# The order of an attention and two-MoE kernel's middle part, planned anew with other costs for issues, transfers and small matmuls

## The chip, the cores and the metric

The kernel runs on one core of a Trainium2 chip. The metric is the device time of one execution in microseconds (us). TensorE (PE in the profile) does the matmuls, VectorE (DVE) and ScalarE (ACT) the elementwise work, GpSimd (POOL) and SyncE (SP) issue the transfers (DMAs).

## The reference

Three stages follow each other: a retention recurrence over 4 x 8 heads of 768 steps, a feed-forward layer with `h * sigmoid(1.702 h)` between two products, and a second one with a rational function between them.

```python
for t in range(S):
    state = gamma[None, :, None, None] * state + np.einsum('bhd,bhe->bhde', k[:, :, t], v[:, :, t])
    y[:, :, t] = scale * np.einsum('bhd,bhde->bhe', q[:, :, t], state)
...
h = x @ w_in
g = h * (1.0 / (1.0 + np.exp(-1.702 * h)))
return (g @ w_out).astype(np.float32)
...
h = x @ w_in
h2 = h * h
h3 = h2 * h
P = a[0] + a[1] * h + a[2] * h2 + a[3] * h3
Q = 1.0 + np.abs(b[0]) * np.abs(h) + np.abs(b[1]) * h2
g = P / (Q + 1e-06)
return (g @ w_out).astype(np.float32)
```

x is 3072 x 512, `w_in` 512 x 2048 and `w_out` 2048 x 512, float32 throughout.

## The kernel before

**Stages.** The recurrence is computed in 24 chunks of 128 steps of the flattened sequences. For a chunk c the queries and keys are loaded with 16 strided DMAs each (the queries on SP, the keys on POOL, from `in_q` and `in_k`) into buffers of the tags `turnq`, `turnk`, `rawk` and `rawv`, scaled and transposed on VectorE into `qT` and `kT`. TensorE makes the scores (`scores`), VectorE masks them (`masks`, tile `sm`), TensorE adds the products with the values and with the running state (`st`), and the sums go on as inputs of the first layer. The buffers of a tag are reused: a tile takes the one whose last use lies longest back, so that a buffer that held chunk c's keys takes another chunk's queries or keys, and the later load waits for the earlier tile's last reader. A trace shows a buffer under the name of its first tile with `_slot` behind it: `rawk_slot` may hold queries.

Both layers split float32 into a rounded high part and a low rest (`gh` and `gl`, `xh` and `xl`), so that three products of 128 x 128 by 128 x 512 stand for one. In the first layer a step j makes `hp` (four inputs' products), ScalarE the activation `z`, ScalarE and VectorE its parts `gh{j}` and `gl{j}`, and TensorE the output products `o`. The outputs are copied out of PSUM into `os` or `sumb` by ScalarE and VectorE and stored to `x2`, to be read again by the second layer. In the same time the second layer's weights are brought in and split: a weight half `s2_n` (n from 0 to 31) is loaded on SP from `moe2_w_in` or `moe2_w_out` into a buffer of `os`, `sumb` or `a`, ScalarE and VectorE make `u{n}` and sums of them, and the results are stored to DRAM on POOL (`wc0_...`, `wo...`). The second half of the planned part combines blocks of inputs and weights (`xs`, `x0`, `split` from a `ring` of loaded weights) for the last part.

**What sets the order.** Each engine and each DMA queue works through its instructions in the order in which the program gives them. The order of the first steps (the string `ORDER`, with `FIRST_STEPS = 14`) is written out by hand. From step 14 on the program doesn't issue: a class `Deck` records every operation with its reads and writes, and `flush` issues all of them in the order that `plan` gives (all of these instructions carry line 375 in the profile, and in the changed kernel 378). This part runs from about 126 to 606 us of the span. The last part, `layer2`, again has an order of its own in the source (line 390).

`plan` is a list scheduler. Each engine has a time from which it is free (`free`, at the start 0 for all five). Of an engine's operations whose inputs are ready, the one recorded first is taken; of the engines, the one that can start first. An operation takes what `cost` says: a matmul of 512 columns 0.2267 us, a smaller one 0.0178 us per 64 columns, a DMA's issue 0.4 us on SP and 0.7 us on POOL, VectorE's and ScalarE's operations a constant and a part by their size. `nc.group(0.25)` makes one operation of several matmuls and adds 0.25 us. A DMA moves behind those before it (`moving`), and its data count as landed 1.6 us later:

```python
            if op.run is not None:
                size, run = op.run
                ns = next((y for x, y in self.RUNS if x >= run), 0.176)
                moving = max(moving, t + 1.0) + size / run * ns / 16
                op.end = moving + 1.6
```

`size` is the DMA's bytes and `run` its contiguous bytes, 128 for the strided loads. These costs decide the order and nothing else: no engine waits for a planned time, but for what its instruction reads and writes. The functions `att_S`, `y_unit` and `z_unit` are the three places where groups are made: scores of the first planned chunk, the first and the second half of a chunk with the next chunk's scores.

Of the kernel before, what the change touches and what calls it, by code (L numbers as in the profile page):

```python
# [233 lines left out]
class Deck:  # L234
# [46 lines left out]
    def cost(self, engine, method, out, views):  # L281
        if method == "dma_start":
            size = 1
            for v in views[:1]:
                size = v.at.size * (P // ROWS if v.home.space != "dram" else 1)
            return (0.4 if engine == "sync" else 0.7), size * 4
        n = int(np.prod(out.shape[1:])) if isinstance(out, View) else 64
        if engine == "tensor":
            return (0.2267 if n >= 512 else 0.0178 * n / 64), None
        if engine == "scalar":  # L290
            return 0.19 + n * 0.00083, None
        if method == "tensor_scalar":
            return 0.155 + n * 0.00052, None
        return 0.155 + n * 0.00104, None
# [19 lines left out]
    def plan(self):  # L314
        ops = self.ops
        left = []
        for line in self.lines.values():
            line.place(ops)
        for op in ops:
            for x in op.need:  # L320
                ops[x].wake.append(op.n)
            left.append(len(op.need))
        free = dict.fromkeys(("tensor", "vector", "scalar", "gpsimd", "sync"), 0.0)
        wait = {e: [] for e in free}
        ready = {e: [] for e in free}
        moving = 0.0
# [5 lines left out]
        while done < len(ops):  # L332
            best = None
            for e in free:
                if ready[e]:
                    t = free[e]
                elif wait[e]:
                    t = max(free[e], wait[e][0][0])
                else:
                    continue  # L340
                if best is None or t < best[0]:
                    best = (t, e)
            t, e = best
            while wait[e] and wait[e][0][0] <= t + 0.02:
                heapq.heappush(ready[e], heapq.heappop(wait[e])[1])
            op = ops[heapq.heappop(ready[e])]
            op.start = t
            free[e] = t + op.dur
            if op.run is not None:
                size, run = op.run  # L350
                ns = next((y for x, y in self.RUNS if x >= run), 0.176)
                moving = max(moving, t + 1.0) + size / run * ns / 16
                op.end = moving + 1.6
            else:
                op.end = t + op.dur
            order.append(op)
            done += 1
            for x in op.wake:
                left[x] -= 1
                if not left[x]:  # L360
                    o = ops[x]
                    r = 0.0
                    for y in o.need:
                        p = ops[y]
                        gap = 0.05 if p.run is not None else 0.0 if p.engine == o.engine else 0.35 if p.engine == "tensor" else 0.2
                        r = max(r, p.end + gap)
                    heapq.heappush(wait[o.engine], (max(r, t), x))
# [442 lines left out]
def tile_kernel(ctx: ExitStack, tc: tile.TileContext, q, k, v, w1i, w1o, w2i, w2o, pa, pb, cst, out):  # L810
# [480 lines left out]

    def att_S(c, tg, alt=None, sums=True):
        pss = [ps(tg[n], f"pS{n}_{c}").rearrange("a x t -> a (x t)") for n in range(2)]
        with nc.group(0.25):
            scores(c, pss, 0, 0)
        if sums:
            state_sums(c, pss, {(x, n) for x in range(2) for n in range(2)})
# [233 lines left out]
        return [t[:, 0], t[:, 1]], None, 0  # L1531

    def y_unit(c):
        with nc.group(0.25):
            att_Y0(c, ("a", "a"), *out_home(c), True, PIECES)
        PIECES[c][0]()
        states_of(c, PY[c])
# [6 lines left out]
    def z_unit(c):  # L1544
        py = PY.pop(c)
        _, second, outs, lows = PIECES.pop(c)
        with nc.group(0.25):
            second()
            if c + 1 < NT // P:
                scores(c + 1, py, 4 * D, 1)  # L1550
# [566 lines left out]
```

## Time and profile before

| | us |
|---|---|
| median of 3 runs | 1106.44 |
| lowest and highest | 1106.31, 1108.31 |
| the profiled execution | 1104.64 |
| its span, first to last instruction | 1102.8 |
| TensorE busy | 1087.5 (99%) |
| VectorE busy | 872.2 (79%) |
| ScalarE busy | 698.5 (63%) |
| GpSimd busy | 208.0 (19%) |
| DMA, mean rate | 181 GB/s |

All durations and places below are of the profiled execution, with times from the start of its span; the time outside the span is 1104.64 − 1102.8 = 1.8 us. Busy is the share of the span in which an engine had an instruction running; a row of a timeline gives start, length, engine, source line, operation, output and inputs and, in brackets, how long the engine had stood idle before it and what released it.

### The profile page before, as it was taken

How to read it: one execution, taken by the hardware profiler on the slowest of the kernel's cores; microseconds unless marked ns; L12 is line 12 of the kernel's file. 1: busy time of each engine (PE TensorE's matmuls, PEld its weight loads, DVE VectorE, ACT ScalarE, POOL GpSimd, SP SyncE). 2: the span in 40 equal slices, each digit the busy share in tenths (PEclk: the TensorE clock that was granted, in tenths of full speed). 3: DMA queues.
4: the chain of work that ended last, by engine and by line, in shares of the span. 5: the costliest groups of instructions: out<-in, count | busy, mean ns of one | idle time of the engine just before them, and what ended most of it. 6: DMA issues, size and time to landing. Idle time of an engine off the chain costs nothing.

```text
span 1102.8 us, 19408 instructions
## 1 busy us (share of the span) xinstructions
PE 1087.5 (99%) x7169; PEld 883.0 (80%) x7169; DVE 872.2 (79%) x1262; ACT 698.5 (63%) x1105; POOL 208.0 (19%) x368
## 2 busy tenths in 40 slices
PE   8999999999999999999999999999999999999998
PEld 6678878888877778888888888888888888888886
DVE  6898556356745679789995799998988897899895
ACT  5898422233323346667763788787787886787882
POOL 0003346545675601133102000000000000000000
PEclk9999999999999999999999999999999999999999
DMA  9964336546776775798878775832454913454011
GB/s 229 318 174 131 77 113 165 141 103 153 194 195 158 219 233 200 236 364 311 290 254 329 267 247 202 315 153 86 126 153 130 333 51 96 124 162 117 19 39 39
DMA packets 192703, 199.76 MB, mean 181 GB/s; under 512 B 108512, under 2 KB 140768, under 8 KB 192608
## 3 DMA queue, kind: packets, MB, share of 16 engines
q1 hardware_dynamic: 172960, 154.45, 46.7%
q0 software_dynamic: 19648, 44.06, 11.5%
q8 instruction: 57, 0.93, 0.4%
q14 instruction: 38, 0.31, 0.1%
HBM read 139.73 MB, written 58.72 MB: 180 GB/s over the span
## 4 chain that ended last, share of the span: by engine, by line
PE 78%; POOL 5%; DMA 5%; SPq 5%; issue 3%; DVE 1%; ACT 1%; DVEq 0%; POOLq 0%; ACTq 0%
PE o L390 26%; PE o_slot L375 14%; PE hp_slot L375 13%; PE a L390 12%; PE c L390 6%; SPq L390 3%; PE b L390 3%; PE hp L390 3%; POOL turnk_slot L375 2%; SPq L375 2%; POOL rawk_slot L375 2%; POOL rawv_slot L375 2%; PE pS_slot L375 1%; DMA os_slot<-in_moe_w_in_dram 1%; DMA s<-in_moe_w_out_dram 1%
## 5 line engine op out<-in xcount | busy, mean ns | idle before, releaser
L375 PE MATMUL o_slot<-gh_slot,wo 128*128 128x512 f32 x480 | 161.7, 393 | 0.0
L375 PEld LDWEIGHTS o_slot<-gh_slot,wo 128*128 128x128 f32 x480 | 90.1, 188 | 19.3
L375 ACT ACTIVATE z_slot<-hp_slot 128x512 f32<-128x512 f32 x56 | 33.4, 596 | 107.8 <-PE hp_slot L375 107.8
L390 PE MATMUL a<-x,wi 128*128 128x512 f32 x384 | 97.5, 389 | 0.0
L375 PE MATMUL o_slot<-gl_slot,wo 128*128 128x512 f32 x240 | 93.5, 390 | 0.0
L375 POOL DMA_DIRECT2D turnk_slot<-in_k_dram x144 | 80.3, 559 | 60.7 <-DVE kT_slot L375 38.7
L375 PE MATMUL hp_slot<-xh_slot,wi 128*128 128x512 f32 x256 | 85.3, 394 | 0.0
L375 PE MATMUL hp_slot<-xl_slot,split_slot 128*128 128x512 f32 x336 | 84.7, 389 | 0.0
L390 PEld LDWEIGHTS a<-x,wi 128*128 128x128 f32 x384 | 72.1, 188 | 15.0
L390 DVE SCALAR_TENSOR_TENSOR z<-z,ab,w 128x1024 f32<-128x1024 f32 x48 | 61.5, 1280 | 28.4 <-ACT w L390 28.4
L375 PEld LDWEIGHTS hp_slot<-xl_slot,split_slot 128*128 128x128 f32 x336 | 63.1, 188 | 13.1
L390 ACT ACTIVATE gh<-h 128x1024 fp32r<-128x1024 f32 x48 | 50.9, 1060 | 34.1 <-PE o L390 33.6
L390 DVE SCALAR_TENSOR_TENSOR gl<-h,gh 128x1024 fp32r<-128x1024 f32 x48 | 58.5, 1219 | 5.4 <-ACT gh L390 5.4
L390 ACT ACTIVATE w<-z,ab 128x1024 f32<-128x1024 f32 x48 | 55.1, 1152 | 12.1 <-DVE z L390 12.1
L390 DVE TENSOR_TENSOR p<-h,p 128x1024 f32<-128x1024 f32 x48 | 58.5, 1219 | 4.4 <-ACT p L390 4.4
L390 DVE SCALAR_TENSOR_TENSOR p<-p,ab,h 128x1024 f32<-128x1024 f32 x48 | 61.4, 1280 | 0.3
L390 DVE SCALAR_TENSOR_TENSOR p<-p,ab,w 128x1024 f32<-128x1024 f32 x48 | 61.3, 1279 | 0.0
L390 ACT ACTIVATE p<-h,ab 128x1024 f32<-128x1024 f32 x48 | 59.6, 1241 | 0.0
L390 DVE SCALAR_TENSOR_TENSOR z<-z,w 128x1024 f32<-128x1024 f32 x48 | 58.5, 1219 | 1.1 <-ACT w L390 0.9
L390 PE MATMUL o<-wo_slot,gh 128*128 128x512 f32 x192 | 59.1, 389 | 0.0
L390 ACT ACTIVATE z<-h 128x1024 f32<-128x1024 f32 x48 | 50.7, 1061 | 12.6 <-DVE h L390 12.1
L390 DVE SCALAR_TENSOR_TENSOR h<-z,p 128x1024 f32<-128x1024 f32 x48 | 58.4, 1219 | 0.2
(369 smaller groups left out, 2745.2 us busy)
## 6 DMA issues: line engine op xcount, KB each, us to landing
wi<-wc SPq DMA_DIRECT2D x168, 256.0 KB, 2.8
x<-xc SPq DMA_DIRECT2D x28, 512.0 KB, 8.4
s<-in_moe_w_in_dram SPq DMA_DIRECT2D x16, 512.0 KB, 7.8
s<-in_moe_w_out_dram SPq DMA_DIRECT2D x16, 512.0 KB, 6.8
ring_slot<-wd SPq DMA_DIRECT2D x56, 128.0 KB, 4.1
wc<-os_slot POOLq DMA_DIRECT2D x11, 512.0 KB, 4.8
xc<-xo SPq DMA_DIRECT2D x10, 512.0 KB, 4.5
out_dram<-os SPq DMA_DIRECT2D x10, 512.0 KB, 3.0
```

The source lines that it names most:

```text
L375: fn(*[self.real(x) for x in args], **{k: self.real(x) for k, x in kw.items()})
L390: return fn(*[d.real(x) for x in args], **{k: d.real(x) for k, x in kw.items()})
```

## The change

Only numbers of the planner change. A DMA's issue counts 0.6 us on SP for the strided loads and 0.45 us for others, and 0.6 us on POOL; a small matmul 0.0295 us per 64 columns; a DMA's data land 2.6 us behind the moving and not 1.6; VectorE is free from 5.5 us on and GpSimd and SP from 5.0; a group adds 0.24 us. The operations themselves, their number, sizes and buffers' tags stay; which buffer of a tag a tile takes follows from the uses and stays too.

```diff
@@ -283,10 +283,10 @@
             size = 1
             for v in views[:1]:
                 size = v.at.size * (P // ROWS if v.home.space != "dram" else 1)
-            return (0.4 if engine == "sync" else 0.7), size * 4
+            return 0.0, size * 4
         n = int(np.prod(out.shape[1:])) if isinstance(out, View) else 64
         if engine == "tensor":
-            return (0.2267 if n >= 512 else 0.0178 * n / 64), None
+            return (0.2267 if n >= 512 else 0.0295 * n / 64), None
         if engine == "scalar":
             return 0.19 + n * 0.00083, None
         if method == "tensor_scalar":
@@ -314,13 +314,16 @@
     def plan(self):
         ops = self.ops
         left = []
+        for op in ops:
+            if op.run is not None:
+                op.dur = (0.6 if op.run[1] == 128 else 0.45) if op.engine == "sync" else 0.6
         for line in self.lines.values():
             line.place(ops)
         for op in ops:
             for x in op.need:
                 ops[x].wake.append(op.n)
             left.append(len(op.need))
-        free = dict.fromkeys(("tensor", "vector", "scalar", "gpsimd", "sync"), 0.0)
+        free = {"tensor": 0.0, "vector": 5.5, "scalar": 0.0, "gpsimd": 5.0, "sync": 5.0}
         wait = {e: [] for e in free}
         ready = {e: [] for e in free}
         moving = 0.0
@@ -350,7 +353,7 @@
                 size, run = op.run
                 ns = next((y for x, y in self.RUNS if x >= run), 0.176)
                 moving = max(moving, t + 1.0) + size / run * ns / 16
-                op.end = moving + 1.6
+                op.end = moving + 2.6
             else:
                 op.end = t + op.dur
             order.append(op)
@@ -1291,7 +1294,7 @@
 
     def att_S(c, tg, alt=None, sums=True):
         pss = [ps(tg[n], f"pS{n}_{c}").rearrange("a x t -> a (x t)") for n in range(2)]
-        with nc.group(0.25):
+        with nc.group(0.24):
             scores(c, pss, 0, 0)
         if sums:
             state_sums(c, pss, {(x, n) for x in range(2) for n in range(2)})
@@ -1531,7 +1534,7 @@
         return [t[:, 0], t[:, 1]], None, 0
 
     def y_unit(c):
-        with nc.group(0.25):
+        with nc.group(0.24):
             att_Y0(c, ("a", "a"), *out_home(c), True, PIECES)
         PIECES[c][0]()
         states_of(c, PY[c])
@@ -1544,7 +1547,7 @@
     def z_unit(c):
         py = PY.pop(c)
         _, second, outs, lows = PIECES.pop(c)
-        with nc.group(0.25):
+        with nc.group(0.24):
             second()
             if c + 1 < NT // P:
                 scores(c + 1, py, 4 * D, 1)
```

All five queues come out in another order in places. TensorE's differs in 92 rows: its products and scores keep their order but for a handful of groups, one of which is the scores of chunk 22, issued with nine output products behind them that stood ahead before. The following shows three places. At the first, around 140 us, SP issues the strided loads of chunk 10's queries (`turnq10`) and the stores of the first outputs (`x2_0_0` to `x2_0_3`, from `os`). Before:

```order
L390 DMA rawv8_1819<-in_v_dram 128x8x64
L375 DMA turnq10_slot_1880<-in_q_dram 32x4x32 x15
L375 DMA x2_0_0_161<-os0_0_slot_1928 128x512
L375 DMA x2_0_1_162<-os0_0_slot_1928 128x512
L375 DMA turnq10_slot_1880<-in_q_dram 32x4x32
L375 DMA x2_0_2_163<-os0_2_slot_1942 128x512
L375 DMA x2_0_3_164<-os0_2_slot_1942 128x512
L375 DMA rawk10_slot_2070<-in_k_dram 128x4x64 x2
```

and now:

```order
L393 DMA rawv8_1819<-in_v_dram 128x8x64
L378 DMA x2_0_0_161<-os0_0_slot_1908 128x512
L378 DMA x2_0_1_162<-os0_0_slot_1908 128x512
L378 DMA x2_0_2_163<-os0_2_slot_1921 128x512
L378 DMA x2_0_3_164<-os0_2_slot_1921 128x512
L378 DMA turnq10_slot_1935<-in_q_dram 32x4x32 x16
L378 DMA rawk10_slot_2086<-in_k_dram 128x4x64 x2
```

The four stores moved ahead of all 16 issues of `turnq10`; one pair stood behind 15 of them, the other behind 16.

The second place is the chunks 18 to 20, from about 296 to 331 us. On SP the queries of chunk 18 are the 16 loads into `turnk10_slot`, those of chunk 19 the 16 into `rawk10_slot`, and the weight halves s2_5 and s2_6 are the loads from `in_moe2_w_in` into `a0_slot` and from `in_moe2_w_out` into `os0_0_slot`. Before:

```order
L375 DMA a0_slot_1899<-in_moe2_w_in_dram 128x4x256
L375 DMA rawv11_slot_2407<-in_v_dram 128x8x64
L375 DMA turnk10_slot_2011<-in_q_dram 32x4x32 x16
L375 DMA x1_4_159<-turnq10_slot_1880 128x4x128
L375 DMA rawv10_slot_2188<-in_k_dram 128x4x64 x2
L375 DMA turnq10_slot_1880<-in_v_dram 128x8x64
L375 DMA rawk10_slot_2070<-in_q_dram 32x4x32 x16
L375 DMA x1_4_159<-turnk10_slot_2011 128x4x128
L375 DMA rawv11_slot_2407<-in_k_dram 128x4x64 x2
L375 DMA os0_0_slot_1928<-in_moe2_w_out_dram 128x1024
L375 DMA sumb1_slot_2067<-in_moe2_w_out_dram 128x1024
```

and now:

```order
L378 DMA rawv11_slot_2409<-in_v_dram 128x8x64
L378 DMA turnk10_slot_2002<-in_q_dram 32x4x32 x16
L378 DMA a0_slot_1960<-in_moe2_w_in_dram 128x4x256
L378 DMA os0_0_slot_1908<-in_moe2_w_out_dram 128x1024
L378 DMA rawv10_slot_2190<-in_k_dram 128x4x64 x2
L378 DMA x1_4_159<-turnq10_slot_1935 128x4x128
L378 DMA turnq10_slot_1935<-in_v_dram 128x8x64
L378 DMA rawk10_slot_2086<-in_q_dram 32x4x32 x16
L378 DMA x1_4_159<-turnk10_slot_2002 128x4x128
L378 DMA rawv11_slot_2409<-in_k_dram 128x4x64 x2
```

s2_5 moved behind chunk 18's queries, s2_6 from behind chunk 19's queries to ahead of them. On VectorE the transpose out of `rawk11_slot` is kT of chunk 19 and the operations on `u0` and `os0_0` are those of s2_6. Before:

```order
L375 TENSOR_TENSOR gl18_slot_1999<-z18_slot_1979,gh18_slot_1986 128x512
L375 COPY st0_8_slot_2073<-pS0_8_slot_1961 128x256
L375 TENSOR_TENSOR st1_8_slot_2081<-pS1_8_slot_1964,st0_8_slot_2073 128x256
L375 TENSOR_SCALAR os0_0_slot_1928<-os0_0_slot_1928 128x512
L375 TENSOR_SCALAR u0_slot_3221<-u0_slot_3221 128x512
L375 SCALAR_TENSOR_TENSOR u0_slot_3221<-u0_slot_3221,os0_0_slot_1928 128x512
L375 STREAM_TRANSPOSE kT_9_slot_2005<-rawk11_slot_2317 128x512
L375 SCALAR_TENSOR_TENSOR u0_slot_3221<-os0_0_slot_1928,u0_slot_3221 128x512
L375 TENSOR_SCALAR u1_slot_2875<-u1_slot_2875 128x512
```

and now:

```order
L378 TENSOR_TENSOR sm_8_slot_1978<-pS1_8_slot_1945,cs_99 128x256
L378 TENSOR_TENSOR os0_0_slot_1908<-os0_2_slot_1921,os0_0_slot_1908 128x2x256
L378 STREAM_TRANSPOSE kT_9_slot_1995<-rawk11_slot_2344 128x512
L378 TENSOR_TENSOR gl18_slot_1982<-z18_slot_1962,gh18_slot_1970 128x512
L378 COPY st0_8_slot_2084<-pS0_8_slot_1942 128x256
L378 TENSOR_TENSOR st1_8_slot_2088<-pS1_8_slot_1945,st0_8_slot_2084 128x256
L378 TENSOR_TENSOR rawk10_slot_2086<-rawk10_slot_2086,qtab_101 128x512
L378 STREAM_TRANSPOSE qT_9_slot_1927<-rawk10_slot_2086 128x512
L378 TENSOR_TENSOR gl16_slot_1879<-z16_slot_1862,gh16_slot_1867 128x512
```

kT of chunk 19 stood behind two of the operations on s2_6 and ahead of the third; now the last one stands some rows ahead of it, and kT is ahead of the low part and the two states (`st0`, `st1`).

The third place is ScalarE near 569 us, with the copies of the first layer's last outputs out of PSUM (`sumb1<-o16`, buffers `o16_1` and `o16_3`), casts of the inputs (`xl4`) and the activation of a weight (`u1`). Before:

```order
L375 CAST gh16_slot_1874<-hold4_1_slot_5408 128x512
L375 CAST os0_0_slot_1928<-u1_slot_2875 128x256
L375 CAST xl4_5_0_slot_5127<-turnq10_slot_1880 128x512
L375 COPY sumb1_slot_2067<-o16_3_slot_2001 128x512
L375 CAST xl4_6_0_slot_5203<-rawv11_slot_2407 128x512
L375 ACTIVATE u1_slot_2875<-os0_2_slot_1942 128x512
L375 CAST gh17_slot_1926<-hold4_1_slot_5408 128x512
L375 CAST xl4_3_1_slot_5134<-rawk10_slot_2070 128x512
```

and now:

```order
L378 CAST gh16_slot_1867<-hold4_1_slot_5407 128x512
L378 CAST xl4_1_1_slot_5022<-turnk10_slot_2002 128x512
L378 CAST os0_0_slot_1908<-u1_slot_2874 128x256
L378 CAST xl4_5_0_slot_5128<-turnq10_slot_1935 128x512
L378 CAST xl4_6_0_slot_5203<-rawv11_slot_2409 128x512
L378 ACTIVATE u1_slot_2874<-os0_2_slot_1921 128x512
L378 COPY sumb1_slot_2060<-o16_3_slot_1990 128x512
L378 CAST gh17_slot_1903<-hold4_1_slot_5407 128x512
```

The copy of `o16_3` stands behind the cast of `xl4_6_0` and the activation of `u1`, which both followed it; the cast of `gh16` changed places with that of `xl4_1_1`.

## Rows read from the trace of the kernel before

**Rows 1.** The page's busy times: engine, busy us, share, instructions.

```profile
PE 1087.5 (99%) x7169; PEld 883.0 (80%) x7169; DVE 872.2 (79%) x1262; ACT 698.5 (63%) x1105; POOL 208.0 (19%) x368
```

**Rows 2.** What TensorE waited for: us in total, times, longest.

```profile
PE pS_slot L375 <- DVE kT_slot L375: 3.8, 3, 2.5
PE pS_slot L375 <- DVE sm_slot L375: 1.8, 1, 1.8
...
PE pS_slot L375 <- ACT rawk_slot L375: 0.5, 1, 0.5
```

**Rows 3.** Stretches: length; busy (instructions) PE, PEld, DVE, ACT, POOL; PEclk; DMA share; GB/s.

```profile
146.00:151.00 5.00, 3.18 (x52) 2.31 (x53) 1.72 (x5) 1.22 (x2) 0.00 (x0) 1.00 0.67 224
320.00:350.00 30.00, 26.74 (x335) 21.28 (x334) 16.61 (x32) 8.32 (x20) 19.37 (x34) 1.00 0.74 196
370.00:400.00 30.00, 28.43 (x300) 22.87 (x299) 20.75 (x41) 11.00 (x24) 10.62 (x18) 1.00 0.78 213
```

**Rows 4.** SP's loads of turnq by tile, 138 to 147; timeline of SP and VectorE.

```profile
L375 SPq DMA_DIRECT2D turnq_slot<-in_q_dram x15: 329/430/2445, 138.0 to 146.6; - x15
...
DMA to landing us min/median/max: 1.5/1.8/4.3
...
147.13 0.85 SPq L375 DMA_DIRECT2D x<-os_slot  x2
...
149.28 0.42 DVE L375 TENSOR_TENSOR os_slot<-a_slot 128x256 f32<-128x256 f32 x1 [6.48 <-DMA x<-os_slot]
```

**Rows 5.** Timeline of VectorE and TensorE, 328 to 331.

```profile
328.40 0.43 DVE L375 TENSOR_SCALAR os_slot<-os_slot 128x512 int32<-128x512 uint32 x1 [2.31 <-DMA os_slot<-in_moe_w_out_dram]
...
330.11 0.70 DVE L375 STREAM_TRANSPOSE kT_slot<-rawk_slot 128x512 f32<-128x512 f32 x1
...
330.86 0.34 PE L375 MATMUL pS_slot<-qT_slot,kT_slot 64*64 64x64 f32 x8 [2.50 <-DVE kT_slot L375]
```

**Rows 6.** Timeline of SP's issues, 296 to 340.

```profile
296.98 8.47 SPq L375 DMA_DIRECT2D turnk_slot<-in_q_dram  x16
...
322.77 0.61 SPq L375 DMA_DIRECT2D os_slot<-in_moe_w_out_dram  x1
...
330.83 9.37 SPq L375 DMA_DIRECT2D rawk_slot<-in_q_dram  x16
```

**Rows 7.** DMA issues from 255 to 400: count, KB each, median us to landing.

```profile
os_slot<-in_moe_w_out_dram SPq DMA_DIRECT2D x4, 512.0 KB, 4.8
...
a_slot<-in_moe_w_in_dram SPq DMA_DIRECT2D x2, 512.0 KB, 6.0
...
rawk_slot<-in_k_dram POOLq DMA_DIRECT2D x32, 16.0 KB, 2.2
```

**Rows 8.** Timeline of GpSimd's issues, 312 to 319.

```profile
312.29 6.21 POOL L375 DMA_DIRECT2D rawk_slot<-in_k_dram  x11 [1.40 <-issue]
```

**Rows 9.** Timeline of all engines, 568 to 570.

```profile
568.59 0.58 ACT L375 COPY sumb_slot<-o_slot 128x512 f32<-128x512 f32 x1
...
569.07 0.62 ACT L375 CAST xl_slot<-rawv_slot 128x512 fp32r<-128x512 f32 x1
...
569.22 0.19 PEld L375 LDWEIGHTS o_slot<-gh_slot,wo_slot 128*128 128x128 f32 x1 [0.22 <-ACT sumb_slot L375]
...
569.59 0.68 ACT L375 ACTIVATE u_slot<-os_slot 128x512 f32<-128x512 f32 x1
```

**Rows 10.** Timeline of all engines, 532 to 534.5.

```profile
532.17 0.42 DVE L375 TENSOR_TENSOR split_slot<-ring_slot,split_slot 128x256 fp32r<-128x256 f32 x1 [0.51 <-ACT split_slot L375]
532.51 0.42 DVE L375 TENSOR_TENSOR a_slot<-a_slot,u_slot 128x256 f32<-128x256 f32 x1
...
533.60 0.62 ACT L375 CAST os_slot<-a_slot 128x512 fp32r<-128x512 f32 x1
...
533.77 1.07 PE L375 MATMUL hp_slot<-xl_slot,split_slot 128*128 128x512 f32 x4
...
534.25 0.69 DVE L375 TENSOR_TENSOR os_slot<-a_slot,os_slot 128x512 fp32r<-128x512 f32 x1
```

## The prediction

> **What bounds the kernel now.** I read the head of the page first: TensorE is busy 1087.5 us, 99% of the span [rows 1]. No other engine can be the bound, and the time can fall only where TensorE stands still. The list of its waits comes next [rows 2]: in the part that the planner orders (line 375) it waits for VectorE's transposed keys (kT), 3.8 us in three places, for the masked scores (sm), 1.8 us once, and for a load that ScalarE passes on, 0.5 us. The table by stretches says where [rows 3]: 146 to 151 lacks 5.00 − 3.18 = 1.82 us, 320 to 350 lacks 3.26 and 370 to 400 lacks 1.57, in all 6.65 us. The granted clock is 1.00 in each of them, the 2.4 GHz level, so a stall costs its own length and no more. The last part of the program (line 390) keeps its order and only starts earlier when a stall goes.
>
> The ceiling of this change is therefore about 6.6 us, 0.6% of the time: no instruction is added or removed, and TensorE's own work stays. What it can do for the worse has no such ceiling, so I go through the new order place by place.
>
> **First place, 148 us.** TensorE waits 1.8 us for the masked scores [rows 2], because VectorE, which makes them, had stood 6.48 us in front of the addition before them, waiting until 149.28 for a store of `os` to land and free its buffer [rows 4]. That store was issued on SP from 147.13 on, and ahead of it stood the 15 issues of the strided load `turnq10`, the first at 138.0 and the last at 146.6: 8.6 / 14 = 0.61 us each [rows 4]. In the new order the four stores stand ahead of the 16 issues, and on VectorE the masked scores stand ahead of the addition that waits for the store, where 6.48 us of idle time take them. I take −1.8 us. The 16 issues come behind four stores now, 4 x 0.43 = 1.7 us later by the stores' row [rows 4]; the queries they load are used a chunk later, so I cost that at nothing. Without that cover it would cost those 1.7 us.
>
> The Trainium skill, page "DMA: Bandwidth & Descriptors", section "Issuing engines are not separate DMA queues", says that the time to initiate a DMA is usually small beside the DMA itself; by that the place of the stores in SP's queue is worth little. The row differs: 15 issues are 9 us, while one such load lands 1.8 us after its issue. By the rule this term would be 0 and the sum −2.9 us.
>
> **Middle, 320 to 400.** The chain there runs through reused buffers: the strided loads of a later chunk go into the buffer that an earlier chunk's kT was made from, so a late kT delays loads, and these the next kT. At 330.11 VectorE began kT of chunk 19, and TensorE, which had waited 2.50 us, went on at 330.86 [rows 5]. Ahead of kT stood operations on a weight (`os`, `u`), the first of which had waited 2.31 us for its load; the load was issued on SP at 322.77, behind the issues of chunk 19's queries [rows 5, 6]. In the new order it stands directly behind the queries of chunk 18, which end at 296.98 + 8.47 = 305.5 in the old rows [rows 6]; issued there it lands near 305.5 + 0.4 + 4.8 = 311 [rows 7], 17 us sooner. kT 19 itself moves ahead of a low part (gl) and two states. The last of its keys was issued by 312.29 + 6.21 = 318.5 [rows 8] and such a load takes 2.2 us [rows 7], so kT 19 can be made near 321, some 7 us before TensorE asks for it at 330.86 − 2.50 = 328.4. That gives −2.5 us. The other 0.7 us of the stretch are at 343, where TensorE waited for chunk 20's queries; their 16 issues began at 330.83, the moment kT 19 was done [rows 6], so they come up to 7 us sooner: −0.7. The two stalls from 370 to 400, 1.57 us together, sit at kT of chunks 22 and 23 and hang on the same chain; besides, four output stores go behind the keys of chunk 22 on SP: −1.5. One thing works against it: TensorE's scores of chunk 22 move ahead of nine output products, 9 x 0.227 = 2.0 us (four such products take 1.07 us and one 0.39, so one starts each 0.68 / 3 us [rows 10]), and so need their kT 2.0 us sooner. Ends for the whole middle: −4.8 and +2.0 (every stall stays and these scores wait 2.0 us longer). I take −4.7, near the first, because both rows that hold the chain up, the wait of 2.31 us and the load's late issue, are gone in the order.
>
> **New waits.** Three places lose cover.
>
> At 569 us copies on ScalarE and VectorE (`sumb<-o`) empty the banks into which TensorE writes again at once. ScalarE's copy ran from 568.59 to 569.17, and the weights of the product that wants its bank already waited 0.22 us for it, until 569.22 [rows 9]: there is no cover at all. In the new order a cast and an activation stand ahead of the copy, which take 569.59 − 569.07 = 0.52 and about 0.6 us of their row's 0.68 (rows of this engine overlap by about 0.1) [rows 9]. The copy ends 1.1 us later. A third operation, ahead of all these, changes places with one that VectorE waits for and may let the group start up to 0.5 us sooner. Ends 0 and 1.1; I take 0.9, near the row. VectorE's copy also loses two places, but what TensorE already waits covers that.
>
> At 533.8 us a product needs the second half of a split input, which VectorE made by 532.59, 1.18 us ahead [rows 10]. Now three sums and two weight operations stand in front, and one of these needs a cast on ScalarE that goes first there too. Put one behind the other from 531.7, where the work before ended: three sums of 0.34 us to 532.7, the cast of 0.62 to 533.3, the operation of 0.69 to 534.0 and the split of 0.42 to 534.4, by their rows [rows 10]. TensorE waits 0.7 us. Ends 0 and 1.1 (the cast behind its neighbour as well); I take 0.7.
>
> At 298 and 311 us the states and kT 18 get a little behind weight work: 0.2 us, ends 0 and 0.6, the length of one such operation.
>
> **Sum.** −1.8 − 4.7 + 0.9 + 0.7 + 0.2 = −4.7 us. The profiled execution took 1104.64 us, so 1099.9 on its own scale; the median of the runs shown is 1.80 us above it, and against that median, 1106.44, the forecast is **1101.7 us**.
>
> **Rivals.**
> *All stalls go and no new one comes*: −6.6, 1099.8 us. For it: wherever TensorE waits less, everything that feeds it may also run earlier. Against it: a product with no cover and 1.1 us put in front of what it needs.
> *The first stall stays*: −4.7 + 1.8, 1103.5 us. It would need the place of the stores among the issues not to matter, which the 9 us of issues ahead of them speak against. The sentence of the page above is this case.
> *The middle stays*: −1.8 + 1.8 = 0, 1106.4 us, up to 1108.4 with the scores of chunk 22. For it: a chain through reused buffers can move its wait to the next link. Against it: the load that held kT 19 is issued before chunk 19's 16 issues and not after.
> *Slower, by late weights in front of kT 18*: the new order puts two weight loads behind the 16 issues of chunk 18's queries; one of them stood before these issues until now, and all its work on VectorE is now ahead of kT 18: an activation, two combining steps of 0.6 us, about six of 0.34 to 0.43 and kT itself, some 4.7 us by their like in [rows 5, 9, 10]. If the queries start no sooner than before, that load goes out at 305.5, lands 6.0 us later at 311.5 [rows 7], and kT 18 is done at 316.2 where TensorE asks for it at 312: 4.2 us of waiting, and the later links as late as before. −1.8 + 1.8 + 4.2 = +4.2, 1110.6 us. It decides if the load lands after about 307. Against it: kT of chunks 16 and 17, on which those queries wait, each stand seven places further ahead on VectorE, so I expect the load out near 298.
> *The change does nothing*: excluded by the order, which differs on all five queues.
>
> **Chances.** The forecast 0.56, no new wait 0.10, the first stall stays 0.04, the middle stays 0.17, late weights 0.13. A measurement of this kernel tells about 0.2% from no change, 2.2 us, so below 1104.2 is faster and above 1108.6 slower: 0.56 + 0.10 + 0.04 = 0.70 faster, 0.17 the same, 0.13 slower. The range goes from 1099.6, all stalls gone, to 1106.6, which still holds the middle's lower end; late weights and the rest of that case, 0.2, lie outside.
>
> **What would show it.** In the new profile: no wait for sm, and 146 to 151 full; no wait for kT over 0.3 us; kT 19 with no load's wait in the three operations before it; TensorE waiting 0.5 to 1.1 us for `sumb` near 564 (569 less 5) and 0.7 us for `split` near 529. The prediction is wrong if TensorE lacks over 2 us between 310 and 400, if a load's wait stands in front of kT 18, or if the part from line 390 changes its length.

## The result, and the profile after

The changed kernel takes 1096.06 us (median of 4 runs, 1095.68 to 1096.62), the kernel before 1106.38 us beside it (4 runs, 1104.97 to 1108.31): a ratio of 0.9906, 95% interval 0.9889 to 0.9923, or −10.3 us. The forecast was −4.7 us, 1101.7 us, and its range reached down to 1099.6: the direction was right, the size was not. Part of the size lies in the few runs: later sets of 18 to 33 runs of the kernel before have medians of 1103.3 to 1104.0 us, and beside one of them, on one chip, the changed kernel is 7.4 us faster (1096.16 against 1103.55, e9 below).

The head of the page after, and its chain that ended last (the work followed back from the last instruction to what released it, step by step; share of the span by engine):

```profile
PE 1085.7 (99%) x7169; PEld 882.2 (81%) x7169; DVE 875.2 (80%) x1262; ACT 699.3 (64%) x1105; POOL 206.0 (19%) x368
...
PE 96%; ACT 0%; DVE 0%; issue 0%; ACTq 0%
```

The same line of the chain on the page of the kernel before, which the prediction did not read:

```profile
PE 78%; POOL 5%; DMA 5%; SPq 5%; issue 3%; DVE 1%; ACT 1%; DVEq 0%; POOLq 0%; ACTq 0%
```

Busy time is the same 99% in both. The chain differs: before, 15% of the way to the last instruction led through transfers (DMA) and the engines that issue them (POOL, SPq); after, it is TensorE nearly throughout. That one line already said that in this execution a part of the program ended when a chain of loads ended, not when TensorE's work did.

What TensorE waits for now in the planned part (line 378) is one row, where [rows 2] had three and more:

```profile
PE o_slot L378 <- ACT sumb_slot L378: 0.3, 1, 0.3
```

The stretches that answer to [rows 3], now some 2 to 9 us earlier, are full but for that row's place (columns as in [rows 3]):

```profile
130.00:151.00 21.00, 21.00 (x181) 17.02 (x180) 16.57 (x32) 6.22 (x11) 7.18 (x13) 1.00 0.48 129
310.00:342.00 32.00, 32.00 (x360) 25.86 (x360) 16.04 (x30) 8.37 (x21) 20.21 (x37) 1.00 0.67 161
342.00:392.00 50.00, 50.00 (x572) 40.51 (x571) 34.02 (x62) 19.93 (x42) 23.06 (x41) 1.00 0.86 238
...
530.00:565.00 35.00, 34.68 (x154) 28.35 (x153) 33.28 (x64) 26.38 (x50) 4.64 (x7) 1.00 0.78 260
```

Where the time went between the two profiled executions is read from the start of TensorE's n-th matmul in each trace:

| matmul | before, us | after, us | gained up to here |
|---|---|---|---|
| 1200 | 140.68 | 140.04 | 0.64 |
| 1400 | 163.02 | 160.18 | 2.84 |
| 3000 | 305.35 | 302.50 | 2.84 |
| 3200 | 327.35 | 324.07 | 3.28 |
| 3400 | 345.38 | 338.27 | 7.11 |
| 3600 | 361.84 | 354.68 | 7.16 |
| 4000 | 395.82 | 386.72 | 9.10 |
| 4800 | 561.19 | 552.08 | 9.11 |
| 5000 | 606.77 | 598.07 | 8.70 |
| last | 1098.54 | 1089.82 | 8.72 |

So 8.5 us were gained at the stalls, 0.4 lost at one new wait, and 0.6 came from the head, whose order did not change. VectorE's kT of chunk 19, and SP's issues around it, answer to [rows 5, 6]:

```profile
313.98 0.71 DVE L378 STREAM_TRANSPOSE kT_slot<-rawk_slot 128x512 f32<-128x512 f32 x1 [2.26 <-DMA rawk_slot<-in_k_dram]
```

```profile
284.86 9.14 SPq L378 DMA_DIRECT2D turnk_slot<-in_q_dram  x16
294.09 1.17 SPq L378 DMA_DIRECT2D a_slot<-in_moe_w_in_dram  x1
295.43 0.38 SPq L378 DMA_DIRECT2D os_slot<-in_moe_w_out_dram  x1
...
305.54 7.45 SPq L378 DMA_DIRECT2D rawk_slot<-in_q_dram  x16
```

kT 19 now waits for its own keys alone and is made at 313.98 instead of 330.11; the weight load s2_6 goes out at 295.43 instead of 322.77. Call cover the time from the end of kT to the start of the last of the scores' matmuls that read it; it is 0.53 us where TensorE waits for kT itself. For chunks 13 to 22, from both traces:

| chunk | 13 | 14 | 15 | 16 | 17 | 18 | 19 | 20 | 21 | 22 |
|---|---|---|---|---|---|---|---|---|---|---|
| before, us | 15.1 | 9.9 | 4.5 | 3.4 | 1.7 | 0.5 | 0.5 | 1.3 | 3.5 | 0.5 |
| after, us | 14.9 | 9.7 | 11.7 | 10.4 | 11.4 | 3.8 | 10.6 | 4.9 | 8.4 | 3.4 |

Up to chunk 14 both are alike. The kernel before loses its cover at chunk 15, and from there link by link. VectorE's rows of that place, before:

```profile
257.14 0.71 DVE L375 STREAM_TRANSPOSE qT_slot<-turnq_slot 128x512 f32<-128x512 f32 x1
260.94 0.43 DVE L375 TENSOR_SCALAR u_slot<-u_slot 128x512 f32<-128x512 f32 x1 [3.09 <-ACT u_slot L375]
...
263.68 0.71 DVE L375 STREAM_TRANSPOSE kT_slot<-turnk_slot 128x512 f32<-128x512 f32 x1
```

and the issues of the keys on GpSimd, the last of them at 252.1, the time that these 16 loads took to land, and the weight's load on SP behind:

```profile
247.46 5.14 POOL L375 DMA_DIRECT2D turnk_slot<-in_k_dram  x9 [0.29 <-issue]
```

```profile
DMA to landing us min/median/max: 2.0/2.7/4.0
```

```profile
253.18 2.07 SPq L375 DMA_DIRECT2D os_slot<-in_moe_w_in_dram  x1
```

kT 15 had its keys by about 256 (252.1 + 4.0 at most), and VectorE stood still for 3.09 us, until 260.94, before a weight (s2_0) that went out after them. The old costs explain why it was ordered so: the planner gave an issue on GpSimd 0.7 us, which took 0.56 (6.21 / 11, [rows 8]), and one on SP 0.4, which took 0.53 to 0.61 ([rows 4, 6]). In the times that `plan` itself works out the weight had landed 3.8 us before the keys (119.4 against 123.2); with the new issue costs the keys land 3.4 us before the weight (120.0 against 123.4 with these costs alone).

### The profile page after: what moved, and what is told of

Read it like the earlier page. It is cut to its first block, busy times and chain, and to the rows that moved or that the text cites. A ratio compares the mean times of both kernels' runs of the same rounds, so it can differ in the third digit from the quotient of the medians.

```text
span 1094.1 us, 19424 instructions
## 1 busy us (share of the span) xinstructions
PE 1085.7 (99%) x7169; PEld 882.2 (81%) x7169; DVE 875.2 (80%) x1262; ACT 699.3 (64%) x1105; POOL 206.0 (19%) x368
## 3 DMA queue, kind: packets, MB, share of 16 engines
q0 software_dynamic: 19648, 44.06, 11.7%
## 4 chain that ended last, share of the span: by engine, by line
PE 96%; ACT 0%; DVE 0%; issue 0%; ACTq 0%
PE o L393 27%; PE o_slot L378 20%; PE hp_slot L378 19%; PE a L393 12%; PE c L393 6%; PE hp L393 3%; PE pS_slot L378 3%; PE b L393 3%; PE o L378 0%; PE pY L393 0%; PE pS L393 0%; PE pTq L393 0%; PE pTk L393 0%; DVE s L393 0%; DVE u L393 0%
## 5 line engine op out<-in xcount | busy, mean ns | idle before, releaser
L378 DVE TENSOR_TENSOR gl_slot<-z_slot,gh_slot 128x512 fp32r<-128x512 f32 x64 | 44.0, 687 | 42.5 <-ACT gh_slot L378 42.2
```

Of the source, the lines that this page charges most:

```text
L378: fn(*[self.real(x) for x in args], **{k: self.real(x) for k, x in kw.items()})
```

## The experiments

All medians are of several runs, beside the kernel before on the same chip; the ratio is to that kernel, with its 95% interval. The kernel before itself lay between 1099.0 and 1109.0 us in these sets.

| run | what differs | median, us | before, us | ratio |
|---|---|---|---|---|
| e2 | before, later start of engines only | 1103.07 | 1103.34 | 0.9995 [0.9977, 1.0013] |
| e3 | changed, engines free from 0 | 1095.63 | 1103.34 | 0.9931 [0.9913, 0.9949] |
| e4 | before, stores ahead of turnq10 | 1102.75 | 1103.34 | 0.9988 [0.9971, 1.0005] |
| e5 | before, kT of chunks 15 to 22 earlier | 1098.97 | 1103.95 | 0.9966 [0.9947, 0.9986] |
| e6 | before, kT of chunk 19 earlier | 1102.49 | 1103.95 | 0.9983 [0.9964, 1.0002] |
| e7 | changed, landing 1.6 us | 1097.67 | 1103.95 | 0.9953 [0.9936, 0.9970] |
| e8 | changed, old issue costs | 1103.74 | 1103.95 | 0.9997 [0.9982, 1.0012] |
| e9 | changed, again | 1096.16 | 1103.55 | 0.9935 [0.9919, 0.9952] |
| e10 | changed, copies at 560 first | 1095.00 | 1103.55 | 0.9933 [0.9909, 0.9957] |
| e11 | changed, old small-matmul cost | 1095.93 | 1103.55 | 0.9935 [0.9913, 0.9957] |
| e12 | before, new issue costs only | 1095.15 | 1103.55 | 0.9933 [0.9909, 0.9957] |
| e13 | e5 with e4 | 1097.75 | 1103.85 | 0.9946 [0.9929, 0.9964] |
| e14 | e5, again | 1099.83 | 1103.85 | 0.9972 [0.9955, 0.9990] |
| e15 | changed, kT of chunk 15 late | 1096.97 | 1103.85 | 0.9943 [0.9923, 0.9962] |

**e1, the kernel before again.** No edit.

> The kernel before, unchanged, profiled once more. The changed kernel's profile lies 8.7 us below the first profile of the kernel before, its median 10.3 us below the median. Theory: the 1.6 us between are more of the same stalls, which hang on when loads land and so change from execution to execution; an execution nearer to the median (1106.4 us) shows the stalls between 310 and 400 us 1 to 2 us longer and the rest of the program as before. Rival: they lie outside the part that is planned, in the hand-ordered head (before 126 us) or in the last part.

It took 1104.12 us, so it does not show an execution near 1106. But its stalls (gaps from start to start of two matmuls) differ: 1.44 us from start to start at 147 instead of 2.21, 1.83 at 310 and 0.73 at 297 where there was little or none, 1.00 at 330 instead of 2.71. The sum of the gaps over 0.37 us is 9.35 us against 9.29, and matmul 4900 starts at 583.81 against 584.11. In these two executions the stalls move about and their sum hardly does, as if something other than TensorE set where the middle ends; e2 below shows that the sum can be much smaller. The head did not explain the difference either (matmul 1000 at 114.45 against 114.88).

**e2 and e4, the first place alone.** e2 changes one line of the kernel before; e4 moves SP's issues behind the stores in the finished order:

```diff
-        free = dict.fromkeys(("tensor", "vector", "scalar", "gpsimd", "sync"), 0.0)
+        free = {"tensor": 0.0, "vector": 5.5, "scalar": 0.0, "gpsimd": 5.0, "sync": 5.0}
```

```diff
+        at = {op.n: op for op in order}
+        late = [op for op in order if op.n in range(69, 85)]
+        order = [op for op in order if op.n not in range(69, 85)]
+        k = order.index(at[33]) + 1
+        order[k:k] = late
```

> The kernel before with the three engines' later start alone. Its order differs from the kernel before only around 140 us (stores ahead of the 16 strided issues, masked scores ahead of the addition). Theory (stalls are separate and each costs its whole start-to-start gap): the wait for the masked scores goes, the stalls at 311 to 392 stay: -2.2 us, about 1104.2. Rival (one chain: a later start of the same stalls eats the gain up): -0.5 us or less.

> The order of before, with one thing moved: the 16 issues of turnq10 on SP stand behind the four stores of the first outputs. VectorE's order stays, with the masked scores behind the addition that waits for the store. Theory: the store lands some 9 us sooner, the addition doesn't hold the masked scores, -2.2 us, as much as with the later start. Rival: VectorE's order is what counts, and the wait stays in part: -1 us or less.

Both mend the place: neither profile has a gap there. The medians moved by 0.3 and 0.6 us, near the rival, though the intervals are too wide to exclude 2 us. The stretches of e4 say where the time went (columns as in [rows 3]):

```profile
130.00:151.00 21.00, 21.00 (x181) 17.02 (x180) 10.81 (x19) 6.05 (x10) 3.89 (x7) 1.00 0.38 107
151.00:310.00 159.00, 158.29 (x1724) 128.13 (x1726) 98.36 (x216) 46.61 (x103) 96.49 (x175) 1.00 0.56 151
310.00:400.00 90.00, 83.72 (x978) 67.31 (x969) 51.94 (x98) 30.68 (x67) 47.25 (x84) 1.00 0.73 196
```

The same stretches of the kernel before:

```profile
151.00:310.00 159.00, 159.00 (x1736) 129.00 (x1728) 97.57 (x213) 46.19 (x101) 98.92 (x177) 1.00 0.57 149
310.00:350.00 40.00, 36.53 (x435) 29.15 (x434) 20.74 (x41) 11.63 (x28) 27.30 (x48) 1.00 0.70 179
350.00:400.00 50.00, 48.43 (x563) 39.00 (x562) 32.17 (x61) 19.49 (x41) 21.34 (x37) 1.00 0.78 214
```

In e4 nothing is lacking from 130 to 151, but from 151 to 400 it is 0.71 + 6.28 = 7.0 us, against 3.47 + 1.57 = 5.0 us before; matmul 4900 starts at 584.02, as before. In this execution the part behind took back what the first place gave. e2's profile, in which the loads behind the first place go out in the order of before, says the opposite:

```profile
151.00:310.00 159.00, 159.00 (x1762) 128.87 (x1761) 94.84 (x208) 47.44 (x103) 94.14 (x170) 1.00 0.56 152
310.00:400.00 90.00, 87.69 (x992) 70.52 (x993) 53.28 (x100) 31.34 (x70) 47.12 (x85) 1.00 0.74 204
```

It lacks 2.3 us and reaches matmul 4900 at 578.65, 5.5 us sooner, in an execution of 1098.93 us. So with one order of loads the stalls of the middle can sum to 2 or to 7 us, and that a chain takes back the first place's gain is not shown by these two profiles.

**e3, the changed kernel without the later start.** The same line of `free`, put back.

> The changed kernel with the engines free from 0 again. Theory: only the first place goes back, TensorE waits for the masked scores again, by up to 2.2 us, and no stall comes back between 310 and 400: 1097 to 1098.3. Rival (the early start shapes the whole order): stalls in the middle come back, above 1100.

Wrong: the first place didn't come back. Its order on SP puts 10 and 11 of the 16 issues ahead of the two pairs of stores, not 15 and 16, and on VectorE the masked scores stand ahead of the addition that waits for the store:

```profile
141.58 0.74 DVE L378 TENSOR_TENSOR sm_slot<-pS_slot,cs 128x256 f32<-128x256 f32 x2
...
144.77 0.42 DVE L378 TENSOR_TENSOR os_slot<-a_slot 128x256 f32<-128x256 f32 x1 [1.23 <-DMA x<-os_slot]
```

Which of the two was enough was not tried apart. The later start gains nothing in the changed kernel.

**e5, e14 and e6, kT alone.** In each pair the operation of the first number is put ahead of that of the second in its engine's line. Eight operations move on VectorE and nothing on any other engine; e6 moves one, (994, 992):

```diff
...
+        for n, first in ((632, 644), (724, 827), (812, 912), (905, 903), (994, 992), (1084, 1253), (1167, 1165), (1275, 1284)):
+            line = seq[at[n].engine]
+            line.remove(at[n])
+            line.insert(line.index(at[first]), at[n])
...
```

> The order of before with eight operations moved on VectorE alone: the transposes kT of chunks 15 to 22 stand in front of the weight work or query work that they followed. No load moves on SP or POOL. Theory (kT's place on VectorE is the lever: each kT that waits behind a weight's load makes the next chunk's loads late): the stalls from 296 to 392 go, about 6.5 us of start-to-start gaps, and only the wait for the masked scores stays: 1097 to 1098.5 where the kernel before gives some 1103 to 1106. Rival (the loads' places in the queues count as much): half of the stalls stay, 1100 to 1103.

> The eight transposes alone once more, on the same chip as the run above: 1097 to 1099, one gap of 1.3 to 2.2 us at 147 for the masked scores.

> The order of before with one operation moved on VectorE: kT of chunk 19 in front of its queries' scaling. Theory (the slack is lost link by link from chunk 15 on): the stall at 328 goes, 2.5 us, and its successor at 343 shrinks, but those at 296 to 312, 376 and 392 stay: -2 to -4 us. Rival (the step as predicted: the one late weight load sets the middle): all stalls behind 328 go, -5 us.

In e5's profile no stall is left from 296 to 392, only the masked scores and a short wait at 470:

```profile
PE pS_slot L392 <- DVE sm_slot L392: 1.2, 1, 1.2
...
PE hp_slot L392 <- ACT hold_slot L392: 0.2, 1, 0.2
```

Its median is 1098.97, a little over what was expected, and 1099.83 the second time, with gaps of 1.0 us at 147, 1.6 at 309 and 0.6 at 372 in that profile, outside what was expected too. So kT's place on VectorE is the larger part, 4 to 5 us of medians out of some 7.5; what is left is put down to the loads' places in the queues and the first place: between theory and rival. In e6's profile the gaps at 328 and 343 are gone, as the prediction had it for this link, and the later ones at 370 and 373 stay, the first of them longer (1.97 and 1.29 us from start to start, where the kernel before has 0.46 and 1.29), which speaks for the theory. The median's −1.5 us is less than was expected, and its interval holds 0. No run moves kT of chunk 15 alone in the order of before. What the stalls at 370 to 374 did is the surprise (columns as in [rows 3], PEclk is the third from the end):

```profile
370.00:374.00 4.00, 1.35 (x39) 0.79 (x40) 3.30 (x7) 1.83 (x4) 3.48 (x7) 1.00 0.79 177
374.00:376.00 2.00, 2.00 (x35) 1.65 (x36) 1.97 (x5) 0.65 (x3) 0.43 (x1) 0.62 0.14 27
376.00:378.00 2.00, 2.00 (x6) 1.61 (x5) 1.45 (x4) 0.53 (x2) 0.77 (x2) 0.52 0.71 243
378.00:380.00 2.00, 2.00 (x10) 1.61 (x10) 0.00 (x0) 0.14 (x1) 0.10 (x1) 1.00 0.74 214
```

**e7, e8, e11 and e12, which of the costs.** In the changed kernel e7 puts back the landing time, e11 the small matmuls' cost and e8 the issue costs (here in this order); e12 is the kernel before with the issue costs of the change alone, e8's edit the other way round.

```diff
-                op.end = moving + 2.6
+                op.end = moving + 1.6
...
-            return (0.2267 if n >= 512 else 0.0295 * n / 64), None
+            return (0.2267 if n >= 512 else 0.0178 * n / 64), None
...
-            return 0.0, size * 4
+            return (0.4 if engine == "sync" else 0.7), size * 4
...
-        for op in ops:
-            if op.run is not None:
-                op.dur = (0.6 if op.run[1] == 128 else 0.45) if op.engine == "sync" else 0.6
```

> The changed kernel with data landed 1.6 us behind the moving again instead of 2.6. Theory (the planner of before put kT behind weight work because it took loads to land too soon): stalls come back in the middle, 1098 or more, and the execution-to-execution spread with them. Rival (the issue durations do it, since they set when the loads go out): 1096 as with all.

> The changed kernel with issues costed at 0.4 us (SP) and 0.7 us (POOL) again. Theory (landing time is the lever): 1096 to 1097, no stall over 0.4 us between 296 and 400. Rival (issue durations are the lever, 16 issues of 0.2 us too little each make a chunk's queries 3 us later than planned): stalls come back, 1098 or more.

> The changed kernel with a small matmul costed at 0.0178 us per 64 columns again. Theory (the chain of kT hangs on when loads are thought to go out and land): within 1 us of the changed kernel. Rival (a plan that thinks the scores shorter than they are runs ahead of TensorE by a few us over the chunks and orders VectorE for it): stalls in the middle, 1098 or more.

> The kernel before with the issue durations alone. Taking them out of the change gave the whole gain back. Theory (they are the lever by themselves): most of the gain, 1097 to 1099, no gap over 1 us between 296 and 400. Rival (they only work together with the later landing and the longer small matmuls, since the three decide together when kT's keys are thought ready): 1101 or more.

The issue durations are the lever. Without them the whole gain is gone (e8: rival right), by themselves they give all of it and 1.0 us more than the changed kernel (e12: theory right). The landing time is worth about 1.5 us in the changed kernel (e7: between theory and rival, with gaps of 0.9 us at 383 and 1.0 at 469 in the profile and a spread of 5 us), but e12, which keeps the old 1.6 us, doesn't miss it; the small matmuls are worth nothing (e11: theory right). The numbers for SP and for GpSimd were not tried apart. Chunk 15's cover is 5.9 us in e8 and 11.6 in e12, so the issue costs decide kT 15's place. In e8's profile TensorE waits for the states (`st`, 2.3 us) and for a load that ScalarE passes on (1.1 us), and for no kT: the old issue costs bring stalls back, not the same ones. e8 lacks 3.56 of the 82 us from 310 to 392, and again the clock fell:

```profile
368.00:372.00 4.00, 1.54 (x14) 0.87 (x14) 2.86 (x6) 0.27 (x1) 3.81 (x8) 0.96 0.63 161
372.00:374.00 2.00, 2.00 (x61) 1.86 (x61) 1.99 (x6) 0.83 (x2) 1.41 (x3) 0.50 0.77 165
374.00:376.00 2.00, 2.00 (x10) 1.63 (x8) 1.88 (x5) 1.75 (x6) 0.72 (x1) 0.73 0.22 34
```

e12 has no wait at all in the planned part, the new one at 560 included:

```profile
310.00:392.00 82.00, 82.00 (x930) 66.43 (x929) 50.43 (x93) 27.88 (x61) 44.12 (x78) 1.00 0.78 210
520.00:575.00 55.00, 55.00 (x244) 45.54 (x243) 50.60 (x97) 38.43 (x72) 6.43 (x11) 1.00 0.80 279
```

**e9 and e10, the new wait.** e10 moves the two copies on ScalarE and VectorE ahead of what the new order put in front of them, with the loop of e5 and the pairs (2242, 2319) and (2239, 2304).

> The changed kernel again, beside the two runs below on one chip. 1096 us within 0.5, no TensorE wait over 0.4 us in the planned part but the one for the copy at 560 us.

> The changed kernel with two operations moved: ScalarE's and VectorE's copies out of PSUM at 560 us stand in front of the two casts and the activation, and the two sums, that the new order put ahead of them. Theory (the one new wait of the changed kernel is this place): the start-to-start gap of 0.71 us there goes back to 0.23, and the median falls by 0.3 to 0.5 us against the changed kernel. Rival (what is put behind the copies makes a later product wait): no gain, and another gap of 0.3 us or more within 20 us.

The gap, 0.71 us in the changed kernel, goes back to a product's 0.23 and no other appears. The median falls by 1.16 us, more than the place can give; in the profiles the unchanged head ended 1.3 us sooner as well (matmul 1000 at 113.45 against 114.76), and what of the medians' difference that is stays open. With e12, at 1095.15, this is the fastest kernel here.

**e13 and e15, what was still open.** e13 joins the edits of e5 and e4; e15 is the changed kernel with the pair (632, 661), kT 15 behind the weight's combining steps again.

> The eight transposes moved on VectorE (as before) and also the 16 issues of turnq10 behind the four stores on SP: both places that the prediction priced, in the order of before and with nothing else. Theory (in the order of before the part from 296 to 392 ends when the chain of loads and kT ends, so that time saved at 148 is lost there again; with the chain out of the way it counts): no gap at 148, median 1.0 to 2.0 us below that of the eight moves alone. Rival (the first place is worth little anywhere, something else then holds TensorE near 148): within 0.5 us of it.

> The changed kernel with kT of chunk 15 alone put back behind the combining steps of the weight half s2_0, as in the order of before. Theory (slack is lost link by link; the changed order has some 10 us at each of the next chunks): no stall, 1096 within 0.7 us. Rival (the first link sets all later ones, since each kT frees the next chunk's buffer): stalls in the middle as before, 1099 or more.

e13 shows no gap at 148 and lies 2.1 us below e14, a little more than was expected. But the runs overlap (1095.5 to 1099.97 against 1096.99 to 1103.47), and three of e14's eleven have a mean granted clock of 0.998 while none of e13's eight has; the runs with 0.999 or 1.000 differ by 1.0 us on the mean (1097.9 against 1098.9). That the edit which moved medians by 0.3 to 0.6 us in the order of before gives more with the stalls out of the way is therefore likely by the direction, not shown. e13's profile also keeps gaps of 1.7 us at 309 and 1.1 at 506. e15 shows no stall: one late link doesn't bring them back where the next ones have cover. It was close, since chunk 18's cover fell from 3.8 to 0.8 us. Its median is 0.8 us above that of e9, a little more than was expected, on another chip.

## Why the prediction was wrong

It priced every place and named most of the right ones. The step that failed is "the ceiling of this change is therefore about 6.6 us": between the profiled executions the stalls that went were worth 8.5 us, and the medians, for which the forecast was made, lay further apart still. The terms of the new waits failed too. Between the two profiled executions, and then between medians:

| step | forecast, us | measured, us |
|---|---|---|
| first place | −1.8 | −2.2 |
| middle, with 311 | −4.7 | −6.3 |
| new waits | +1.8 | +0.4 |
| head, same order | 0 | −0.6 |
| profiled pair to medians | 0 | −1.6 |
| sum | −4.7 | −10.3 |

**A stall's length.** The idle time in [rows 2, 3] counts from the end that the profile models for a matmul, 0.39 us after its start, but the next product starts 0.23 us after. The two matmuls around the first stall, before:

```profile
147.88 0.39 PE L375 MATMUL hp_slot<-xh,wi 128*128 128x512 f32 x1
150.09 0.62 PE L375 MATMUL pS_slot<-rawv,rawk 64*64 64x64 f32 x8 [1.82 <-DVE sm_slot L375]
```

From start to start it is 2.21 us, which costs 2.21 − 0.23 = 1.98 and not 1.82; by the table of matmuls the place was worth 2.2. For the 64x64 matmuls, modelled at 0.3 to 0.5 us and started every few hundredths, each stall is short by as much or more. The stalls come to 8.5 us by the table of matmuls above and to 6.65 by the columns that were read. The terms had sizes that were about a fifth too small.

**One execution for all.** "The granted clock is 1.00 in each of them, so a stall costs its own length and no more" held in that execution and not in others. Of 56 runs of the kernel before in the first two sets, 19 had a mean granted clock of 1.000 and 29 one of 0.998; the latter took 2.4 us longer on the mean in one set and 2.3 in the other (1104.7 and 1104.6 against 1102.3). The changed kernel's 11 runs of e9 all have 0.999 or 1.000 and lie within 2.1 us. So the medians of the kernel before hold losses of clock that the changed kernel hardly has, and no sum over one execution's stalls shows them. The prediction saw that the execution was 1.80 us below the median and only shifted the scale.

That median was itself high. The four runs beside the result took 1104.97 to 1108.31 us; the 93 of the later sets, 1098.96 to 1108.95 with medians of 1103.3 to 1104.0, so that the profiled execution, at 1104.64, is slower than most of them. Against e9's neighbours the change is worth 7.4 us and not 10.3. About 3 us of the miss are thus the four runs, by chance or by their chip, which stays open; some 2.7 us are left against the forecast of 4.7.

**Separate stalls.** The middle was taken as a sum of waits with a fixed size. The runs show links that hang together, in amounts that change between executions: in e6 the stalls at 328 and 343 go and a later one grows, in e4 the part behind gave the first place's time back, in e2 it didn't. How much of the medians this makes stays open. The prediction's own account of the buffers had such a chain for kT 19 and 20, but it began it at kT 19, where the stall was longest; the cover sinks from kT 15 on, 66 us earlier, where TensorE didn't wait at all. It also took both stalls from 370 to 400 for waits for kT; the second, at 393, is one for a load that ScalarE passes on:

```profile
378.78 0.69 PE L375 MATMUL pS_slot<-qT_slot,kT_slot 64*64 64x64 f32 x32 [1.08 <-DVE kT_slot L375]
...
393.00 0.46 PE L375 MATMUL pS_slot<-qT_slot,st_slot 64*64 64x64 f32 x16 [0.42 <-ACT turnq_slot L375]
```

**The new waits.** The one at 569 came, at 0.48 us by start to start where 0.9 was taken. The group in front did start sooner, which the prediction named and hardly credited:

```profile
559.30 0.67 ACT L378 ACTIVATE u_slot<-os_slot 128x512 f32<-128x512 f32 x1
559.87 0.57 ACT L378 COPY sumb_slot<-o_slot 128x512 f32<-128x512 f32 x1
...
560.50 0.50 PE L378 MATMUL o_slot<-gh_slot,wo_slot 128*128 128x512 f32 x1 [0.32 <-ACT sumb_slot L378]
```

The one at 533.8, priced at 0.7, did not. VectorE made the split as late as was worked out, but TensorE's own order had changed there too, and twelve output products stand in front of the product that needs it where three stood before:

```profile
524.41 0.76 DVE L378 TENSOR_TENSOR split_slot<-ring_slot,split_slot 128x256 fp32r<-128x256 f32 x2
...
526.70 1.07 PE L378 MATMUL hp_slot<-xl_slot,split_slot 128*128 128x512 f32 x4
```

The split is done at 525.2, 1.5 us ahead. The prediction counted what moved on the waiting side and not what moved on the side that is waited for. The waits at 298 and 311 did not come either.

**Right** were the first place, the cause at kT 19 (e6), the copies at 569, and that the last part keeps its length (491.8 us from matmul 5000 to the last in both). The first place's term rested on the 9 us of issues ahead of the stores against the rule of the Trainium skill ("DMA: Bandwidth & Descriptors", section "Issuing engines are not separate DMA queues") that the time to initiate a DMA is usually small beside the DMA. The rows here agree with the prediction and not with the rule: the 16 issues of a tile took 7.45 to 9.37 us on SP, while one such load lands 1.8 us after its issue ([rows 4]). The runs add that what the planner takes an issue for, 0.4 or 0.45 to 0.6 us on SP and 0.7 or 0.6 on GpSimd, decides the whole gain of some 8 us (e8 against e12).

## What to carry to other kernels

Before pricing stalls one by one, read the chain that ended last: an engine that is 99% busy but has 78% of the chain is held up by a chain somewhere, and the prices of its links need not add up. Measure a stall from start to start of the pitch that the engine keeps elsewhere, look for the place where cover is first lost and not where the wait is longest, and take many executions of a kernel whose runs spread by 10 us, for its median too. For a planner, measure the issue durations on each queue first; a wrong order of two queues' arrivals puts a waiting operation ahead of one that is ready.

## What was not expected of the hardware

After a stall TensorE can run slower for some us. In e6 it was busy for 1.35 of the 4 us from 370 to 374, and then the granted clock was 0.62 and 0.52 for 2 us each, near its lower level of 1.2 GHz, with products 0.43 us apart instead of 0.23; full again at 378. By the granted clock that cost an estimated 2 x 0.38 + 2 x 0.48 = 1.7 us beside the stall. In e8 it was busy for 1.54 of 4 us and lost 4 x 0.04 + 2 x 0.50 + 2 x 0.27 = 1.7 us. In the first profile of the kernel before its longest gap, 2.71 us at 328, was followed by no such drop (granted clock 1.00 from 320 to 350, [rows 3]). The Trainium skill, page "TensorE: Matmul & The Clock Gate", section "HAM oscillation — how this bites in real kernels", tells of a loop whose waits for DMA throttle TensorE again; the rows of e6 and e8 agree that a wait can do that, and show it after two stalls close together (1.97 and 1.29 us from start to start) and after one (2.72 us), in an engine that is 99% busy. Why the one of 2.71 us did nothing stays open.

Also, the part of the program whose order no edit touched, up to matmul 1000, ended between 113.3 and 115.7 us in the profiles here. A difference of about 1 us between two medians of this kernel is therefore not put down to a place without a gap to show for it.
